# Dividing P by the row sum in the softmax's rescale, and folding the value sum straight into the projection's input, in a two-layer decode attention kernel

One core of a Trainium2 chip. The metric is the device time of one launch in microseconds (us), as the median of several runs.

## The reference, cut to what matters

Two identical layers of attention over a K/V cache and a small gated FFN, for 4 batch entries with one token each. The second layer reads the same caches and weights again.

```
B, Sq, D = 4, 1, 512;  Hq, Hkv, Sk, Dh = 32, 8, 8192, 128
def A(x, k_cache, v_cache, wq, wo):
    q = (x @ wq) as [B, Hq, 1, Dh]; k, v repeated from 8 to 32 heads
    p = softmax(q k^T * Dh**-0.5);  return (p v) as [B, 1, Hq*Dh] @ wo
x = x + A(layernorm(x), ...);  x = x + ffn(layernorm(x), ...)      # twice
```

K and V are 67 MB each. The kernel's slots (below) hold 11 to 15 MB of them, so nearly all of K and V is streamed twice.

## The kernel before

K and V come in units of 1 MB into 11 slots (later 15, when the slots of wq come free). The SP queue issues the loads in a fixed list, `ORDER`: `K` is the next K unit, `a330` the V unit of layer 0, batch 3, group 3, half 0, `b...` the same for layer 1, `c...` a V unit that both layers use. A load whose slot isn't free blocks all loads behind it. A built-in plan (`Plan.run`) takes the length of every step from a number in the source, decides in which order each engine gets its instructions and which slot a load takes, and the kernel is then emitted in that order. `PL.add(engine, us, function, dependencies, priority)` adds a step.

A K unit is transposed on VectorE (DVE, 2.31 us) and multiplied on TensorE (PE, 32 small matmuls and as many weight loads, 1.1 to 1.9 us in the traces). When all K units of one layer and batch are done, the softmax runs, and only then the V units of this layer and batch can be used and their slots be given back. "(0, 3)" stands for the pass of layer 0, batch 3 from here on.

The softmax, cut (the four blocks of scores each have their own maximum; `alpha` corrects for the common one):

```
al = PL.add("act", 0.3, g6, [s] + ex, CHAIN)             # alpha = exp(...)
def g7():                                                # rescale P, 4 DVE instructions
    for a in range(4):
        seg = pblk(q)[:, :, a, :]
        op("dve", lambda e: e.tensor_scalar(seg, seg, alpha[:, q, a:a + 1], None, op0=ALU.mult), ...)
s = PL.add("dve", 1.14, g7, [al], CHAIN)
for f in range(2):                                       # transpose P on PE, copy back
    t_ = PL.add("pe", 1.02, tr, [s, t_], CHAIN, take=f"{n}t{f}", n=16)
    evs.append(PL.add("dve" if f else "act", 0.68 if f else 1.03, ev, [t_], CHAIN, free=f"{n}t{f}"))
p_ready[(l, b)] = PL.add("act", 0.01, lambda: None, evs, CHAIN)
# beside this path: w1 (row sums, spread to 32 columns), w2 (PE matmul with ones), w3 (reciprocal -> invL)
inv_ready[(l, b)] = PL.add("dve", 0.35, w3, [s], CHAIN, free=n + "l")
```

The fold of a V group, cut:

```
op("dve", lambda e: e.transpose(blk, blk), ...)
op("dve", lambda e: e.tensor_reduce(osum[:], diag, AX.X, ALU.add), ...)
op("dve", lambda e: e.tensor_tensor(oT[:, l, heads, b], osum[:], invL[:, q, heads], ALU.mult), ...)
n = PL.add("dve", 0.17 if direct else 0.88, nm, [prev, inv_ready[(l, b)]], CHAIN, free=tag)
```

Of the kernel before, what the change touches and what calls it, by code (L numbers as in the profile page):

```python
# [5 lines left out]
ALU = mybir.AluOpType  # L6
AX = mybir.AxisListType
BF16 = mybir.dt.bfloat16
FP32 = mybir.dt.float32
# [10 lines left out]
class _Sync:  # L20
# [57 lines left out]
    def op(self, engname, fn, reads=(), writes=(), sig=True):  # L78
        self._wait(engname, self._need(reads, writes))
        ins = fn(self.eng[engname])  # L80
        if sig:
            self.count[engname] += 1
            ins.then_inc(self.prog[engname], 1)
            val = self.count[engname]
        else:
            val = self.count[engname] + 1
        self._record(engname, (self.prog[engname], val), reads, writes)
        return ins
# [184 lines left out]
NP = 2  # L273
# [7 lines left out]
def bass_interleave_layers__gqa_block_cached__swiglu_ffn__decode_kernel(  # L281
# [17 lines left out]
    REP = Hq // G  # L299
# [15 lines left out]
    with ExitStack() as es:  # L315
# [9 lines left out]
        qT1 = sb("qT1", [P, Hq * B], BF16)  # L325
        qT2 = sb("qT2", [P, Hq], BF16)
        ident = sb("ident", [P, P], BF16)
        selL = sb("selL", [P, 32], FP32)
        selw = sb("selw", [P, 32], FP32)
        invL = sb("invL", [P, NP, 32], FP32)  # L330
        xrow = pp[0:B, 0, 0:D]
        xlast = pp[0:B * NQ, 0, 0:P]
        onesm = sb("onesm", [P, P], FP32)
# [13 lines left out]
        lsum = sb("lsum", [P, NP, 4], FP32)  # L347
        gm = sb("gm", [P, 1], FP32)
        gl = sb("gl", [P, 1], FP32)
        osum = sb("osum", [P, REP], FP32)  # L350
        alpha = sb("alpha", [P, NP, 4], FP32)
        wl = sb("wl", [P, 4], FP32)
        m4 = sb("m4", [32, 4], FP32)
# [40 lines left out]

        def setup_late():
            for j in range(4):
                op("dve", lambda e: e.tensor_scalar(selL[32 * j:32 * (j + 1), :],
                                                    ident[32 * j:32 * (j + 1), 32 * j:32 * (j + 1)],
                                                    float(D), None, op0=ALU.mult),
                   reads=["ident"], writes=["selL"])  # L400

        def pk(q):
            return [f"pp{q}_{a}" for a in range(4)]
# [19 lines left out]
        def pbk(key):  # L423
            return PL.bank[key]
# [149 lines left out]
        scores_free = [None]  # L574
        p_free = {k: None for k in range(NP)}
        p_ready = {}
        inv_ready = {}

        def k_pair(u, ld, prio, prev):
            _, l, b, g, cp = u  # L580
# [37 lines left out]
        def softmax(l, b, lastq, prio):  # L618
            q = pb_of[(l, b)]
            n = f"s{l}{b}"  # L620
            ex, mx = [], None
            for a in range(4):
                def m(a=a):
                    op("dve", lambda e: e.tensor_reduce(negm[:, q, a:a + 1], bank(a), AX.X, ALU.max, negate=True),  # L624
                       reads=[f"pb{a}"], writes=[f"negm{q}_{a}"])

                def x(a=a):
                    op("act", lambda e: e.activation(pblk(q)[:, :, a, :], bank(a).rearrange("p (t j) -> p t j", j=32),  # L628
                                                     ACTF.Exp, bias=negm[:, q, a:a + 1], scale=1.0,
                                                     accum_out=lsum[:, q, a:a + 1]),  # L630
                       reads=[f"pb{a}", f"negm{q}_{a}"], writes=[f"pp{q}_{a}", f"lsum{q}_{a}"] + (pt(q) if a == 0 else []))
                mx = PL.add("dve", 0.7, m, [lastq], CHAIN)
                ex.append(PL.add("act", 0.8, x, [mx] + (p_free[q] or []), CHAIN))
            scores_free[0] = ex

            def g1():
                for c in range(4):
                    op("dve", lambda e: e.tensor_reduce(m4[:, c:c + 1], negm[32 * c:32 * (c + 1), q, :], AX.X, ALU.min),
                       reads=[f"negm{q}_{a}" for a in range(4)], writes=["m4"])
                for c in range(4):  # L640
                    op("dve", lambda e: e.tensor_reduce(gm[32 * c:32 * (c + 1), :], m4[:], AX.X, ALU.min),
                       reads=["m4"], writes=["gm"])
            s = PL.add("dve", 1.41, g1, [mx], CHAIN)

            def g6():
                op("act", lambda e: e.activation(alpha[:, q, :], negm[:, q, :], ACTF.Exp, bias=gm[:], scale=-1.0),  # L646
                   reads=[f"negm{q}_{a}" for a in range(4)] + ["gm"], writes=[f"alpha{q}"])
            al = PL.add("act", 0.3, g6, [s] + ex, CHAIN)

            def g7():  # L650
                for a in range(4):
                    seg = pblk(q)[:, :, a, :]
                    op("dve", lambda e: e.tensor_scalar(seg, seg, alpha[:, q, a:a + 1], None, op0=ALU.mult),  # L653
                       reads=[f"pp{q}_{a}", f"alpha{q}"], writes=[f"pp{q}_{a}"])
            s = PL.add("dve", 1.14, g7, [al], CHAIN)
            evs = []
            t_ = None
            for f in range(2):
                def tr(f=f):
                    bk = pbk(f"{n}t{f}")  # L660
                    stg = bank_bf(bk)
                    for t in range(8):
                        blk = f * 8 + t
                        op("pe", lambda e: e.matmul(stg[:, t * P:(t + 1) * P], lhsT=pp[:, q, blk * P:(blk + 1) * P],  # L664
                                                    rhs=ident[:], is_transpose=True, start=True, stop=True),
                           reads=pk(q) + ["ident"], writes=[f"pb{bk}"], sig=(t == 7))

                def ev(f=f):
                    bk = pbk(f"{n}t{f}")
                    src = bank_bf(bk).rearrange("p (t k r) -> p k t r", t=8, r=REP)  # L670
                    dst = pp[:, q, f * 1024:(f + 1) * 1024].rearrange("p (k t r) -> p k t r", t=8, r=REP)
                    if f == 0:
                        op("act", lambda e: e.activation(dst, src, ACTF.Copy), reads=[f"pb{bk}"], writes=[f"pt{q}_{f}"])  # L673
                    else:
                        op("dve", lambda e: e.tensor_copy(dst, src), reads=[f"pb{bk}"], writes=[f"pt{q}_{f}"])
                t_ = PL.add("pe", 1.02, tr, [s, t_], CHAIN, take=f"{n}t{f}", n=16)
                evs.append(PL.add("dve" if f else "act", 0.68 if f else 1.03, ev, [t_], CHAIN, free=f"{n}t{f}"))
            p_ready[(l, b)] = PL.add("act", 0.01, lambda: None, evs, CHAIN)

            def w1():  # L680
                op("dve", lambda e: e.tensor_tensor(wl[:], lsum[:, q, :], alpha[:, q, :], ALU.mult),
                   reads=[f"lsum{q}_{a}" for a in range(4)] + [f"alpha{q}"], writes=["wl"])
                op("dve", lambda e: e.tensor_reduce(gl[:], wl[:], AX.X, ALU.add), reads=["wl"], writes=["gl"])
                op("dve", lambda e: e.tensor_scalar(selw[:], selL[:], gl[:], None, op0=ALU.mult),  # L684
                   reads=["selL", "gl"], writes=["selw"])
            s = PL.add("dve", 0.6, w1, [al, s], CHAIN)

            def w2():
                bk = pbk(n + "l")
                op("pe", lambda e: e.matmul(ps[:, bk * BW:bk * BW + 32], lhsT=onesm[:], rhs=selw[:], start=True, stop=True),  # L690
                   reads=["onesm", "selw"], writes=[f"pb{bk}"])
            s = PL.add("pe", 0.58, w2, [s], CHAIN, take=n + "l", n=8)

            def w3():
                bk = pbk(n + "l")
                op("dve", lambda e: e.reciprocal(invL[:, q, :], ps[:, bk * BW:bk * BW + 32]),
                   reads=[f"pb{bk}"], writes=[f"invL{q}"])
            inv_ready[(l, b)] = PL.add("dve", 0.35, w3, [s], CHAIN, free=n + "l")

        opj_n = [0]  # L700
        opj_free = [None]
# [15 lines left out]
        def v_group(l, b, g, lds, prios):  # L717
# [49 lines left out]

            def nm():
                bk = pbk(tag)
                got = ps[:, bk * BW:bk * BW + REP]  # L770
                if not direct:
                    blk = ps[:, bk * BW:bk * BW + 256]
                    op("dve", lambda e: e.transpose(blk, blk), reads=[f"pb{bk}"], writes=[f"pb{bk}"])  # L773
                    diag = bass.AP(tensor=blk.tensor, offset=blk.offset, ap=[[blk.ap[0][0], P], [1, REP], [32 + REP, 8]])
                    op("dve", lambda e: e.tensor_reduce(osum[:], diag, AX.X, ALU.add), reads=[f"pb{bk}"], writes=["osum"])  # L775
                    got = osum[:]
                op("dve", lambda e: e.tensor_tensor(oT[:, l, g * REP:(g + 1) * REP, b], got,  # L777
                                                    invL[:, q, g * REP:(g + 1) * REP], ALU.mult),
                   reads=[f"pb{bk}", f"invL{q}", "osum"], writes=[f"oT{l}_{g}"])
            n = PL.add("dve", 0.17 if direct else 0.88, nm, [prev, inv_ready[(l, b)]], CHAIN, free=tag)  # L780
            if l == 0 or b == B - 1:
                wdep = [w_load[f"wo{g * REP // (Hq // 4)}"]] if l == 0 else []
                return prev, oproj(l, g, [n, opj_free[0]] + wdep + normed.get((l, g), []), prios[1])
# [281 lines left out]
```

## Time and profile before

| | before |
|---|---|
| time, median of 3 runs | 640.53 us (639.56 to 641.21) |
| span of the profiled run | 637.9 us |
| DMA, mean over the span | 257.31 MB, 403 GB/s |
| busy: PE, DVE, ACT | 63%, 64%, 6% |

How to read it: the DMA engines are busy nearly all the time and no compute engine is. So time is lost only where the stream of loads stops or slows, and before its start and after its end. The prediction shows the lines for this. What it doesn't show is the softmax that will matter. Here it is from the timeline of the kernel before (start, length, engine, line, operation, output and inputs, in brackets the idle time before and what ended it):

```profile
460.08 0.30 ACT L646 ACTIVATE alpha<-negm,gm 128x4 f32<-128x4 f32 x1
461.00 1.10 DVE L653 TENSOR_SCALAR pp<-pp,alpha 128x512 bf16<-128x512 bf16 x4
463.16 0.33 SPq L92 DMA_DIRECT2D pool<-in_A_v_cache_dram  x1
464.69 0.69 DVE L675 COPY pp<-ps 128x1024 bf16<-128x1024 bf16 x1
465.49 1.06 PE L746 MATMUL ps<-pool,pp 128*32 128x256 bf16 x32 [0.83 <-ACT pp L673]
466.20 11.36 SPq L92 DMA_DIRECT2D pool<-in_A_k_cache_dram  x6
```

From the end of alpha (460.38) to the first V matmul (465.49) it takes 5.1 us. The load queue SP stands still from 463.49 to 466.20, because its next slot holds a V unit that is waiting for this P. As soon as that V unit is used, SP goes on.

### The profile page before, as it was taken

What the parts mean: (1) busy time and instruction counts of PE and PEld (TensorE: products, weight loads), DVE (VectorE), ACT (ScalarE), POOL (GpSimd) and SP (SyncE); (2) the same over time, 40 slices, a digit from 0 to 9 for tenths busy, and PEclk for the clock granted to TensorE, in tenths of its full rate; (3) what the DMA queues carried; (4) which work ended last, traced back from release to release, by engine and by line L of the source; (5) the groups of instructions that cost most, each with busy time, mean ns of one, the idle gap of its engine ahead of it and who ended that gap; (6) DMA issues with size and microseconds to landing.
All of it is one profiled execution on the core that took longest, in us unless ns stands there. A gap on an engine that the chain in (4) does not pass through costs nothing.

```text
span 637.9 us, 18599 instructions
## 1 busy us (share of the span) xinstructions
PE 401.5 (63%) x8657; PEld 202.0 (32%) x8657; DVE 405.2 (64%) x612; ACT 40.2 (6%) x106; POOL 1.8 (0%) x8
## 2 busy tenths in 40 slices
PE   0376454375686655678565575677656776866676
PEld 0231221123542131145331241343421244721355
DVE  6386853464236958776579765466667864499732
ACT  1000200002000020000100100000100020000200
POOL 1000000000000000000000000000000000000000
PEclk9985585565556686665677677567585578577685
DMA  8999999999989999999999999999999999999991
GB/s 362 420 418 407 407 418 420 418 421 400 388 354 422 420 418 420 421 418 404 417 414 418 420 419 421 419 409 411 417 420 420 403 420 420 420 416 420 421 415 42
DMA packets 41124, 257.31 MB, mean 403 GB/s; under 512 B 3924, under 2 KB 9816, under 8 KB 11096
## 3 DMA queue, kind: packets, MB, share of 16 engines
q1 hardware_dynamic: 41048, 256.14, 97.8%
q8 instruction: 67, 1.10, 0.7%
q14 instruction: 9, 0.07, 0.0%
HBM read 256.12 MB, written 0.00 MB: 402 GB/s over the span
## 4 chain that ended last, share of the span: by engine, by line
DMA 64%; PE 16%; DVE 13%; SPq 3%; issue 2%; ACT 0%
DMA pool<-in_A_k_cache_dram 45%; DMA pool<-in_A_v_cache_dram 12%; DVE pool L589 9%; PE ps L605 8%; DMA wq_sb<-in_A_k_cache_dram 5%; PE ps L746 4%; SPq L92 3%; DMA wq_sb<-in_A_v_cache_dram 3%; PE ps L467 1%; DVE negm L624 1%; DVE wq_sb L589 1%; PE ps L792 1%; PE ps L664 1%; PE ps L845 1%; DVE ps L773 1%
## 5 line engine op out<-in xcount | busy, mean ns | idle before, releaser
L589 DVE STREAM_TRANSPOSE pool<-pool 128x2048 uint32<-128x2048 uint32 x116 | 267.1, 2308 | 88.4 <-DMA pool<-in_A_k_cache_dram 87.9
L605 PE MATMUL ps<-pool,qpad 32*32 32x512 bf16 x3840 | 197.4, 548 | 130.8 <-DVE pool L589 125.6
L605 PEld LDWEIGHTS ps<-pool,qpad 32*32 32x32 bf16 x3840 | 55.5, 110 | 248.4 <-DVE pool L589 185.8
L746 PE MATMUL ps<-pool,pp 128*32 128x256 bf16 x1952 | 100.5, 362 | 37.6 <-DMA pool<-in_A_v_cache_dram 28.9
L746 PEld LDWEIGHTS ps<-pool,pp 128*32 128x32 bf16 x1952 | 56.2, 120 | 76.3 <-DMA pool<-in_A_v_cache_dram 34.9
L773 DVE STREAM_TRANSPOSE ps<-ps 128x256 f32<-128x256 f32 x63 | 28.8, 457 | 67.4 <-PE ps L746 67.1
L628 ACT ACTIVATE pp<-ps,negm 128x512 bf16<-128x512 f32 x32 | 21.6, 686 | 322.8 <-DVE negm L624 300.5
L709 PE MATMUL ps<-oT,wo_sb 128*128 128x4 bf16 x640 | 22.4, 166 | 11.3 <-DVE oT L777 8.4
L709 PEld LDWEIGHTS ps<-oT,wo_sb 128*128 128x128 bf16 x640 | 20.0, 102 | 24.8 <-DVE oT L777 15.8
L624 DVE TENSOR_REDUCE negm<-ps 128x1 f32<-128x512 f32 x32 | 19.9, 683 | 12.4 <-PE ps L605 12.4
L467 PE MATMUL ps<-xnT,wq_sb 128*128 128x4 bf16 x640 | 18.3, 166 | 12.8 <-DMA wq_sb<-in_A_wq_dram 11.5
L467 PEld LDWEIGHTS ps<-xnT,wq_sb 128*128 128x128 bf16 x640 | 17.7, 104 | 15.3 <-DMA wq_sb<-in_A_wq_dram 11.6
L589 DVE STREAM_TRANSPOSE wq_sb<-wq_sb 128x2048 uint32<-128x2048 uint32 x8 | 18.5, 2312 | 1.8 <-DMA wq_sb<-in_A_k_cache_dram 1.8
L605 PE MATMUL ps<-wq_sb,qpad 32*32 32x512 bf16 x256 | 11.8, 492 | 9.1 <-DVE wq_sb L589 9.1
L664 PE MATMUL ps<-ident,pp 128*128 128x128 bf16 x128 | 15.4, 300 | 2.5 <-DVE oT L777 1.1
L453 ACT ACTIVATE lnv<-var,eps_sb 128x4 f32<-128x4 f32 x10 | 3.0, 297 | 221.5 <-DVE var L448 221.5
L664 PEld LDWEIGHTS ps<-ident,pp 128*128 128x128 bf16 x128 | 11.9, 137 | 9.6 <-DVE selw L684 2.9
L775 DVE TENSOR_REDUCE osum<-ps 128x4 f32<-128x32 f32 x63 | 12.1, 192 | 2.2
L777 DVE TENSOR_TENSOR oT<-osum,invL 128x4 bf16<-128x4 f32 x63 | 10.6, 169 | 2.1
L673 ACT ACTIVATE pp<-ps 128x1024 bf16<-128x1024 bf16 x8 | 8.2, 1024 | 30.1 <-PE ps L664 30.1
L845 PE MATMUL ps<-hT,wd_sb 128*128 128x4 bf16 x280 | 8.6, 166 | 1.8 <-issue 1.1
L653 DVE TENSOR_SCALAR pp<-pp,alpha 128x512 bf16<-128x512 bf16 x32 | 9.0, 344 | 1.1 <-ACT alpha L646 1.1
(68 smaller groups left out, 143.4 us busy)
## 6 DMA issues: line engine op xcount, KB each, us to landing
pool<-in_A_k_cache_dram SPq DMA_DIRECT2D x116, 1024.0 KB, 10.2
pool<-in_A_v_cache_dram SPq DMA_DIRECT2D x101, 1024.0 KB, 10.8
wq_sb<-in_A_k_cache_dram SPq DMA_DIRECT2D x8, 1024.0 KB, 14.8
wq_sb<-in_A_v_cache_dram SPq DMA_DIRECT2D x5, 1024.0 KB, 16.2
wq_sb<-in_A_wq_dram SPq DMA_DIRECT2D x1, 4096.0 KB, 20.0
wo_sb<-in_A_wo_dram SPq DMA_DIRECT2D x4, 1024.0 KB, 15.5
wg_sb<-in_B_w_gate_dram SPq DMA_DIRECT2D x2, 896.0 KB, 19.2
wu_sb<-in_B_w_up_dram SPq DMA_DIRECT2D x2, 896.0 KB, 16.9
```

What stands on the lines that cost most here:

```text
L92: ins = self.eng[engname].dma_start(out_ap, in_ap)
L467: op("pe", lambda e: e.matmul(ps[:, bk * BW + h * B:bk * BW + (h + 1) * B], lhsT=wq_sb[:, kt, h * Dh:(h + 1) * Dh], rhs=xnT[:, kt * B:(kt ...
L589: op("dve", lambda e: e.transpose(v, v), reads=keys, writes=keys)
L605: op("pe", lambda e: e.matmul(ps[32 * c:32 * (c + 1), a * BW:(a + 1) * BW], lhsT=qpad[rows, qbuf, es_, g, :], rhs=ap[h][rows, :, es_ // 2, ...
L624: op("dve", lambda e: e.tensor_reduce(negm[:, q, a:a + 1], bank(a), AX.X, ALU.max, negate=True), reads=[f"pb{a}"], writes=[f"negm{q}_{a}"])
L628: op("act", lambda e: e.activation(pblk(q)[:, :, a, :], bank(a).rearrange("p (t j) -> p t j", j=32), ACTF.Exp, bias=negm[:, q, a:a + 1], s ...
L664: op("pe", lambda e: e.matmul(stg[:, t * P:(t + 1) * P], lhsT=pp[:, q, blk * P:(blk + 1) * P], rhs=ident[:], is_transpose=True, start=True ...
L709: op("pe", lambda e: e.matmul(ps[:, OPJ * BW + nq * B:OPJ * BW + (nq + 1) * B], lhsT=wo_sb[:, h, nq * P:(nq + 1) * P], rhs=oT[:, l, h, :], ...
L746: op("pe", lambda e: e.matmul(ps[32 * n:32 * (n + 1), bk * BW:bk * BW + 256], lhsT=pp[:, q, col:col + 32], rhs=v[:, 8 * f:8 * (f + 1), 32 ...
L773: op("dve", lambda e: e.transpose(blk, blk), reads=[f"pb{bk}"], writes=[f"pb{bk}"])
L775: op("dve", lambda e: e.tensor_reduce(osum[:], diag, AX.X, ALU.add), reads=[f"pb{bk}"], writes=["osum"])
L845: op("pe", lambda e: e.matmul(ps[:, bk * BW + nq * B:bk * BW + (nq + 1) * B], lhsT=wd_sb[:, fo, nq * P:(nq + 1) * P], rhs=hT[:, fo * B:(fo ...
```

## The change

The intent: 63 folds lose their multiply by the reciprocal row sum, since P itself is divided by it. For this the row sum must be known before P is rescaled: what stood beside the path now stands on it.

```
-            def g7():
+            def w1():                        # wl = lsum * alpha; gl = sum of wl
+            s = PL.add("dve", 0.38, w1, [al], CHAIN)
+            def w2():                        # matmul(lhsT=sel, rhs=gl): the row's sum on all 4 quadrants
+            s = PL.add("pe", 0.58, w2, [s], CHAIN, take=n + "l", n=8)
+            def w3():                        # il = 1 / sum; alpha = alpha * il; then the rescale as before
...
-            s = PL.add("dve", 1.14, g7, [al], CHAIN)
+            s = PL.add("dve", 1.5, w3, [s], CHAIN, free=n + "l")
... (the old w1, w2, w3 after the transposes are gone, and selL, selw, invL with them)
-                    op("dve", lambda e: e.tensor_reduce(osum[:], diag, AX.X, ALU.add), ...)
-                op("dve", lambda e: e.tensor_tensor(oT[...], got, invL[...], ALU.mult), ...)
-            n = PL.add("dve", 0.17 if direct else 0.88, nm, [prev, inv_ready[(l, b)]], CHAIN, free=tag)
+                    op("dve", lambda e: e.tensor_reduce(dst, diag, AX.X, ALU.add), ...)      # dst is in oT, bf16
+            n = PL.add("dve", 0.17 if direct else 0.68, nm, [prev], CHAIN, free=tag)
```

`ORDER`, the list of loads, stays as it is.

More of the change, by code (lines that the diff above doesn't have):

```diff
@@ L327, in bass_interleave_layers__gqa_block_cached__swiglu_ffn__decode_kernel @@
         ident = sb("ident", [P, P], BF16)
-        selL = sb("selL", [P, 32], FP32)
-        selw = sb("selw", [P, 32], FP32)
-        invL = sb("invL", [P, NP, 32], FP32)
+        sel = sb("sel", [P, P], FP32)
         xrow = pp[0:B, 0, 0:D]
@@ L349, in bass_interleave_layers__gqa_block_cached__swiglu_ffn__decode_kernel @@
         gl = sb("gl", [P, 1], FP32)
-        osum = sb("osum", [P, REP], FP32)
+        il = sb("il", [P, 1], FP32)
         alpha = sb("alpha", [P, NP, 4], FP32)
@@ L396, in setup_late @@
             for j in range(4):
-                op("dve", lambda e: e.tensor_scalar(selL[32 * j:32 * (j + 1), :],
-                                                    ident[32 * j:32 * (j + 1), 32 * j:32 * (j + 1)],
-                                                    float(D), None, op0=ALU.mult),
-                   reads=["ident"], writes=["selL"])
+                rows = slice(32 * j, 32 * (j + 1))
+                d = ident[rows, rows]
+                rep = bass.AP(tensor=d.tensor, offset=d.offset, ap=[[d.ap[0][0], 32], [0, 4], [1, 32]])
+                op("dve", lambda e: e.tensor_copy(sel[rows, :].rearrange("p (k j) -> p k j", j=32), rep),
+                   reads=["ident"], writes=["sel"])
         def pk(q):
@@ L576, in bass_interleave_layers__gqa_block_cached__swiglu_ffn__decode_kernel @@
         p_ready = {}
-        inv_ready = {}
         def k_pair(u, ld, prio, prev):
@@ L648, in softmax @@
             al = PL.add("act", 0.3, g6, [s] + ex, CHAIN)
-            def g7():
+            def w1():
+                op("dve", lambda e: e.tensor_tensor(wl[:], lsum[:, q, :], alpha[:, q, :], ALU.mult),
+                   reads=[f"lsum{q}_{a}" for a in range(4)] + [f"alpha{q}"], writes=["wl"])
+                op("dve", lambda e: e.tensor_reduce(gl[:], wl[:], AX.X, ALU.add), reads=["wl"], writes=["gl"])
+            s = PL.add("dve", 0.38, w1, [al], CHAIN)
+            def w2():
+                bk = pbk(n + "l")
+                op("pe", lambda e: e.matmul(ps[:, bk * BW:bk * BW + 1], lhsT=sel[:], rhs=gl[:], start=True, stop=True),
+                   reads=["sel", "gl"], writes=[f"pb{bk}"])
+            s = PL.add("pe", 0.58, w2, [s], CHAIN, take=n + "l", n=8)
+            def w3():
+                bk = pbk(n + "l")
+                op("dve", lambda e: e.reciprocal(il[:], ps[:, bk * BW:bk * BW + 1]), reads=[f"pb{bk}"], writes=["il"])
+                op("dve", lambda e: e.tensor_scalar(alpha[:, q, :], alpha[:, q, :], il[:], None, op0=ALU.mult),
+                   reads=[f"alpha{q}", "il"], writes=[f"alpha{q}"])
                 for a in range(4):
@@ L678, in softmax @@
             p_ready[(l, b)] = PL.add("act", 0.01, lambda: None, evs, CHAIN)
-            def w1():
-                op("dve", lambda e: e.tensor_tensor(wl[:], lsum[:, q, :], alpha[:, q, :], ALU.mult),
-                   reads=[f"lsum{q}_{a}" for a in range(4)] + [f"alpha{q}"], writes=["wl"])
-                op("dve", lambda e: e.tensor_reduce(gl[:], wl[:], AX.X, ALU.add), reads=["wl"], writes=["gl"])
-                op("dve", lambda e: e.tensor_scalar(selw[:], selL[:], gl[:], None, op0=ALU.mult),
-                   reads=["selL", "gl"], writes=["selw"])
-            s = PL.add("dve", 0.6, w1, [al, s], CHAIN)
-            def w2():
-                bk = pbk(n + "l")
-                op("pe", lambda e: e.matmul(ps[:, bk * BW:bk * BW + 32], lhsT=onesm[:], rhs=selw[:], start=True, stop=True),
-                   reads=["onesm", "selw"], writes=[f"pb{bk}"])
-            s = PL.add("pe", 0.58, w2, [s], CHAIN, take=n + "l", n=8)
-            def w3():
-                bk = pbk(n + "l")
-                op("dve", lambda e: e.reciprocal(invL[:, q, :], ps[:, bk * BW:bk * BW + 32]),
-                   reads=[f"pb{bk}"], writes=[f"invL{q}"])
-            inv_ready[(l, b)] = PL.add("dve", 0.35, w3, [s], CHAIN, free=n + "l")
         opj_n = [0]
@@ L769, in nm @@
                 bk = pbk(tag)
-                got = ps[:, bk * BW:bk * BW + REP]
-                if not direct:
-                    blk = ps[:, bk * BW:bk * BW + 256]
-                    op("dve", lambda e: e.transpose(blk, blk), reads=[f"pb{bk}"], writes=[f"pb{bk}"])
-                    diag = bass.AP(tensor=blk.tensor, offset=blk.offset, ap=[[blk.ap[0][0], P], [1, REP], [32 + REP, 8]])
-                    op("dve", lambda e: e.tensor_reduce(osum[:], diag, AX.X, ALU.add), reads=[f"pb{bk}"], writes=["osum"])
-                    got = osum[:]
-                op("dve", lambda e: e.tensor_tensor(oT[:, l, g * REP:(g + 1) * REP, b], got,
-                                                    invL[:, q, g * REP:(g + 1) * REP], ALU.mult),
-                   reads=[f"pb{bk}", f"invL{q}", "osum"], writes=[f"oT{l}_{g}"])
-            n = PL.add("dve", 0.17 if direct else 0.88, nm, [prev, inv_ready[(l, b)]], CHAIN, free=tag)
+                dst = oT[:, l, g * REP:(g + 1) * REP, b]
+                if direct:
+                    op("dve", lambda e: e.tensor_copy(dst, ps[:, bk * BW:bk * BW + REP]),
+                       reads=[f"pb{bk}"], writes=[f"oT{l}_{g}"])
+                    return
+                blk = ps[:, bk * BW:bk * BW + 256]
+                op("dve", lambda e: e.transpose(blk, blk), reads=[f"pb{bk}"], writes=[f"pb{bk}"])
+                diag = bass.AP(tensor=blk.tensor, offset=blk.offset, ap=[[blk.ap[0][0], P], [1, REP], [32 + REP, 8]])
+                with nc.allow_low_precision(reason="the sum runs in fp32 and is rounded once"):
+                    op("dve", lambda e: e.tensor_reduce(dst, diag, AX.X, ALU.add), reads=[f"pb{bk}"],
+                       writes=[f"oT{l}_{g}"])
+            n = PL.add("dve", 0.17 if direct else 0.68, nm, [prev], CHAIN, free=tag)
             if l == 0 or b == B - 1:
```

## The prediction

> **What bounds the kernel now.** I read the page first, then eight-microsecond and one-microsecond windows, then the timeline around the one place where DMA falls off and at the end, then the timelines of the eight softmaxes. From the page: engine shares, the DMA row of the 40 slices, and the groups of instructions that the change touches.
>
> ```profile
> PE 401.5 (63%) x8657; PEld 202.0 (32%) x8657; DVE 405.2 (64%) x612; ACT 40.2 (6%) x106; POOL 1.8 (0%) x8
> DMA  8999999999989999999999999999999999999991
> DMA 64%; PE 16%; DVE 13%; SPq 3%; issue 2%; ACT 0%
> L773 DVE STREAM_TRANSPOSE ps<-ps 128x256 f32<-128x256 f32 x63 | 28.8, 457 | 67.4 <-PE ps L746 67.1
> L775 DVE TENSOR_REDUCE osum<-ps 128x4 f32<-128x32 f32 x63 | 12.1, 192 | 2.2
> L777 DVE TENSOR_TENSOR oT<-osum,invL 128x4 bf16<-128x4 f32 x63 | 10.6, 169 | 2.1
> L653 DVE TENSOR_SCALAR pp<-pp,alpha 128x512 bf16<-128x512 bf16 x32 | 9.0, 344 | 1.1 <-ACT alpha L646 1.1
> ```
>
> The reader is to see that no compute engine is full over the span, while the DMA engines are at 90% or more in all slices but the first, the twelfth and the last; 64% of the chain is DMA. The kernel streams 257.31 MB. In plain windows the rate is 420 GB/s, so the bytes alone take 612.6 us. The rest of the 637.9 us span is about 1 us before the first byte, 12 us of compute after the last, and some 12 us in which DMA runs below 420. The eight-microsecond windows show where the largest dip is, and the end:
>
> ```profile
> 176.00:184.00 8.00, 5.83 (x162) 4.98 (x162) 2.06 (x10) 0.50 (x2) 0.00 (x0) 0.50 1.02 419
> 184.00:192.00 8.00, 7.20 (x168) 3.23 (x176) 3.59 (x7) 0.00 (x0) 0.00 (x0) 0.57 0.75 284
> 192.00:200.00 8.00, 4.77 (x152) 2.23 (x130) 3.81 (x2) 0.00 (x0) 0.00 (x0) 0.85 1.01 423
> 616.00:624.00 8.00, 3.40 (x106) 2.78 (x106) 2.38 (x9) 0.00 (x0) 0.00 (x0) 0.81 0.87 358
> ```
>
> Columns after the length: busy PE, weight load, DVE, ACT, POOL, then clock, DMA share, GB/s. Between 185 and 190 us the one-microsecond windows give 229, 205, 229, 98 and 303 GB/s: 5 - 1064/420 = 2.5 us of DMA lost. It is the only hole where the queue ran dry in the middle (the other dips, at 357 to 397 GB/s, have a DMA share near 1 and lie beside the weight loads with their shorter rows). 621 to 626 loses another 2.6 us while the last transfers drain. The hole comes from the first chain: attention, FFN and query of batch 0 must finish before the K units of its second layer can be used; until then the slots are full and no load can be issued. Its timeline:
>
> ```profile
> 177.58 0.47 DVE L773 STREAM_TRANSPOSE ps<-ps 128x256 f32<-128x256 f32 x1 [2.52 <-PE ps L746]
> 178.08 0.19 DVE L775 TENSOR_REDUCE osum<-ps 128x4 f32<-128x32 f32 x1
> 178.31 0.17 DVE L777 TENSOR_TENSOR oT<-osum,invL 128x4 bf16<-128x4 f32 x1
> 178.53 0.64 PE L433 MATMUL ps<-xx,onesm 128*128 128x32 f32 x2 [1.00 <-DVE oT L777]
> ```
>
> The second layer norm (L433) takes the PSUM bank that this fold gives back, so the fold is on the path here. The tail looks as follows.
>
> ```profile
> 620.34 0.17 DVE L777 TENSOR_TENSOR oT<-osum,invL 128x4 bf16<-128x4 f32 x1
> 624.11 1.05 PE L746 MATMUL ps<-wq_sb,pp 128*32 128x256 bf16 x16 [4.07 <-DMA wq_sb<-in_A_v_cache_dram]
> 626.70 0.47 DVE L773 STREAM_TRANSPOSE ps<-ps 128x256 f32<-128x256 f32 x1 [6.20 <-PE ps L746]
> 627.63 0.17 DVE L777 TENSOR_TENSOR oT<-ps,invL 128x4 bf16<-128x4 f32 x1
> ```
>
> PE stood idle 4.07 us for the last V loads: the end is set by the stream, not by the softmax before it (597.7 to 605.8 us).
>
> **What the Trainium skill says.** "Perfetto Trace Analysis", Identifying Performance Opportunities: time is won on the most-contended engine. Here that is DMA, and the change touches no byte of it. "DMA: Bandwidth & Descriptors", Bandwidth, gives 425 GB/s for a 16 MB load; this trace has 420 to 424 in full windows, so there is no reserve. "VectorE: DVE Perf Modes", The TRN2 errata, says that an instruction has a fixed cost that small operands don't amortize; the trace agrees, since the 128x4 multiply takes 169 ns and a 128x128 cast only 273. So removing an instruction is worth its fixed cost, and an added 128x1 one costs about as much.
>
> **The change, part by part.**
> 1. Fold. 63 multiplies by the reciprocal sum go (L777). Starts are 0.23 us apart after the reduce, so a fold shrinks from 0.90 us (start of L773 to end of L777) to 0.69: 0.21 x 63 = 13 us of DVE time, 3% of its busy 405. I take the reduce into bf16 to cost the same 192 ns. The one direct group swaps a 167 ns multiply for a copy that I estimate at 135 (the 128x16 cast from PSUM, L959): 0.03 us on the tail. The multiply at 627.43 was not what the last projection waited for (the direct one at 627.63 was), so the tail gains no more.
> 2. Sum and reciprocal. Per softmax, selw (242 ns) goes and the reciprocal shrinks from 128x32 to 128x1. From 343 ns for 32 elements and 503 for 56, 6.7 ns an element, one element makes about 135 ns. A 128x4 multiply of alpha is added, 156 ns like the other 128x4 operations. Net over 8 softmaxes: -(242 + 208 - 156) x 8 = -2.4 us of DVE. The setup copies replace four 170 ns operations at about 12 us, while wq is still landing: free.
> 3. Chain. The sum now stands before the rescale of P. Added between alpha and the first rescale, without contention: two DVE operations 0.35 us (603.87 to 604.22 in the last softmax), a hop 0.05, the fp32 matmul with its return 0.68 (as L433 to L440 in the tail), reciprocal with spacing 0.17, alpha multiply 0.20: **1.45 us** later P, eight times. Contended it is more: DVE has a gap of 0.7 us between the two halves, where a K transpose of 2.31 us can slip in, and the matmul can stand behind a K unit of up to 1.95 us. I expect 1.5 to 3.5 us.
> 4. Given back. From the end of alpha to the last copy of transposed P the eight softmaxes take 13.1, 8.8, 3.5, 10.6, 6.5, 5.0, 7.0 and 3.9 us now. In at least three (the first, second and fourth) the second transposed half comes only after the reciprocal, whose bank it reuses or behind which it stands (155.40 reciprocal, 155.82 second half). With the sum first, its bank is free before the halves need theirs, so there P should be no later and may be earlier.
> 5. Order. Instructions are issued in the order of a built-in plan, which is computed anew from the changed step times, with the load order kept. Which V unit stands before which chain step, and which slot a load takes, can change by a unit (1 to 2.5 us) at any place.
>
> On the path: the hole should close by the 0.2 us of its fold; tail -0.03; every other saving of part 1 lies beside the stream. The longer softmaxes free V slots later by 1.5 to 3.5 us, but a load lands 10 to 11 us after issue (page, part 6), thus about four 2.5 us units are queued when SP has to wait, and the last softmax has 17 us of queue and 4 us of idle PE behind it. Sum of what I can place: -0.2 us. I add +0.6 for the reordering, because the load order was evidently tuned for the old step times and an arbitrary shift is likelier to open a hole than close one: 640.5 - 0.2 + 0.6, rounded to **640.9 us**.
>
> **Rivals.**
> (a) The stream hides everything: 640 to 641. For it: DMA share, 4 us of PE idle at the end, only one hole.
> (b) Later P opens holes. Each microsecond by which P comes later than the queue lasts is lost. For it: SP did run dry once, and DVE is above 90% busy in the K stretches (7.5 of 8 us), which stretches a chain with more DVE visits. Against it: none of the eight softmaxes is followed by a hole now; the dip at 185 hangs on the q chain. One or two new holes of 2 us: 643 to 646.
> (c) The lighter DVE and earlier banks bring the q chain forward and close the hole: at most 2.5 us, with smaller dips (433, 508 us) another 1: 637. Against it: the chain starts at 165.0, after the projection that waited for a weight load, and passes through V matmuls that wait for DMA.
> (d) DVE is the real bound, and its 15 us count in full: 625. Against it: DVE waits for K loads 87.9 us in total; I give this almost nothing.
>
> **Range and chances.** (a) has most of the weight, (b) about a quarter, (c) a fifth. Low end 637.5 (hole closed), high end 645 (two holes). A change of over 2% is 12.8 us: for a gain DVE would have to be the bound, or for a loss five or more holes. Faster 0.01, same 0.96, slower 0.03.
>
> **What would show it.** Folds without the multiply, 0.69 us long, and DVE busy near 390 us: part 1 and 2. From alpha to the first rescale 1.5 to 3.5 us more: part 3. Second halves of P close behind the first, so that the three long softmaxes aren't longer: part 4. DMA still at about 403 GB/s over the span, one hole near 185 of about 2.3 us, 12 us of tail: the sum. I am wrong if a hole of several microseconds follows a softmax, if the hole at 185 goes or doubles, or if the tail is no longer reached with PE waiting for DMA.

## The result, and the profile after

The changed kernel takes 643.28 us (642.06 to 643.48, 4 runs), the kernel before in the same comparison 640.87 (4 runs). The ratio is 1.0036 with a 95% interval of 1.0015 to 1.0057: slower, by less than half a per cent. Ratios are the mean time of one kernel's runs over that of the other's of the same rounds, so not quite the ratio of the medians quoted.

Three lines of the page after, the ones for busy time, the DMA row of the 40 slices, and the fold's reduce:

```profile
PE 397.5 (62%) x8657; PEld 203.6 (32%) x8657; DVE 394.3 (61%) x549; ACT 40.2 (6%) x106; POOL 1.8 (0%) x8
DMA  8999999999989999999999999999989999999991
L773 DVE TENSOR_REDUCE oT<-ps 128x4 bf16<-128x32 f32 x63 | 12.2, 194 | 2.1
```

DVE is busy 10.9 us less, nearly all of it the multiply that went (10.6), and the reduce costs the same with a bf16 output. But the DMA row has a second 8 in the middle, in the 30th slice. The eight-microsecond windows there (last three columns: granted clock, DMA share, GB/s), first before, then after:

```profile
464.00:472.00 8.00, 3.69 (x99) 2.06 (x105) 5.67 (x4) 1.02 (x1) 0.00 (x0) 0.92 1.01 420
472.00:480.00 8.00, 4.53 (x104) 1.38 (x88) 5.99 (x3) 0.00 (x0) 0.00 (x0) 0.71 1.01 419
```

```profile
464.00:472.00 8.00, 4.86 (x66) 2.60 (x50) 5.74 (x9) 1.02 (x1) 0.00 (x0) 0.50 0.81 336
472.00:480.00 8.00, 3.88 (x116) 2.10 (x112) 3.30 (x3) 0.00 (x0) 0.00 (x0) 0.92 0.82 325
```

I summed the DMA packets of both traces in one-microsecond bins and counted what is missing to 420 GB/s. The hole at 185 to 190 us is there in both, 2.47 us before and 2.44 after. A new one lies at 469 to 475, with 3.4 us lost. As all loads come in the same order, one can also ask when the same number of megabytes had arrived, counted from the start of each span (packets of the load queue):

```
MB arrived            8     96    120    168    192    200    248    256
after minus before  +0.13  +0.06  +0.76  +0.74  +1.11  +4.31  +3.60  +3.65 us
```

Of the 3.7 us between the two spans, 3.2 come in one step between 192 and 200 MB, which is the new hole. The two are level up to 96 MB; 0.7 us comes between 96 and 120 MB and 0.7 goes again between 200 and 248, in small dips.

What happened in the hole, from the timeline of the kernel after:

```profile
461.66 0.30 ACT L644 ACTIVATE alpha<-negm,gm 128x4 f32<-128x4 f32 x1
462.71 1.90 PE L603 MATMUL ps<-pool,qpad 32*32 32x512 bf16 x32 [3.77 <-DVE wl L649]
464.55 0.58 PE L656 MATMUL ps<-gl,sel 128*128 128x1 f32 x2
464.74 0.33 SPq L92 DMA_DIRECT2D pool<-in_A_v_cache_dram  x1
465.64 1.14 DVE L667 TENSOR_SCALAR pp<-pp,alpha 128x512 bf16<-128x512 bf16 x4
467.80 2.31 DVE L587 STREAM_TRANSPOSE pool<-pool 128x2048 uint32<-128x2048 uint32 x1 [1.02 <-DMA pool<-in_A_k_cache_dram]
470.04 0.65 DVE L689 COPY pp<-ps 128x1024 bf16<-128x1024 bf16 x1
470.17 1.91 PE L603 MATMUL ps<-pool,qpad 32*32 32x512 bf16 x32 [1.44 <-DVE pool L587]
472.00 1.65 PE L740 MATMUL ps<-pool,pp 128*32 128x256 bf16 x32
472.19 8.79 SPq L92 DMA_DIRECT2D pool<-in_A_k_cache_dram  x6
```

From the end of alpha (461.96) to the first V matmul it is now 10.0 us in place of 5.1. The sum's matmul (L656) stands behind a K unit on PE. After the rescale, the copy of the second half of P (L689) stands behind a K transpose on DVE, and that transpose lets a K unit onto PE ahead of the V matmul. The additional 4.9 us are 3.1 up to the rescale, 0.7 from there to the last copy, and 1.2 to the V matmul (each rounded). SP waits from 465.07 to 472.19, 7.1 us in place of 2.7, and the queued loads run out. What ended this wait shows in the list of SP's waits from 440 to 482 us (us in total, times, longest):

```profile
SPq L62 <- PE ps L603: 22.3, 6, 7.1
SPq L62 <- PE ps L740: 12.4, 9, 2.5
```

The wait of 7.1 us ended with a K unit (L603, done at 472.08) and not with a V unit. While P is not there, the V units keep their slots, and the first slot to come free is that of a K unit which landed behind them: it was transposed at 467.80 and multiplied at 470.17, ahead of the V units on PE. In the kernel before, a V unit came first, and its slot ended the wait.

### The profile page after: what moved, and what is told of

Its sections match the earlier page's. It is cut to its first block, busy times and chain, and to the rows that moved or that the text cites. A ratio compares the mean times of both kernels' runs of the same rounds, so it can differ in the third digit from the quotient of the medians. Undisturbed runs are those within 1.5% of the kernel's fastest.

```text
span 641.6 us, 18536 instructions
## 1 busy us (share of the span) xinstructions
PE 397.5 (62%) x8657; PEld 203.6 (32%) x8657; DVE 394.3 (61%) x549; ACT 40.2 (6%) x106; POOL 1.8 (0%) x8
## 4 chain that ended last, share of the span: by engine, by line
DMA 64%; PE 17%; DVE 13%; SPq 3%; issue 2%; ACT 0%
DMA pool<-in_A_k_cache_dram 45%; DMA pool<-in_A_v_cache_dram 12%; DVE pool L587 10%; PE ps L603 9%; DMA wq_sb<-in_A_k_cache_dram 5%; PE ps L740 4%; SPq L92 3%; DMA wq_sb<-in_A_v_cache_dram 3%; DVE negm L622 1%; PE ps L466 1%; DVE wq_sb L587 1%; PE ps L787 1%; PE ps L678 1%; PE ps L840 1%; PE ps L703 0%
## 5 line engine op out<-in xcount | busy, mean ns | idle before, releaser
L603 PE MATMUL ps<-pool,qpad 32*32 32x512 bf16 x3840 | 193.0, 537 | 135.0 <-DVE pool L587 116.8
L603 PEld LDWEIGHTS ps<-pool,qpad 32*32 32x32 bf16 x3840 | 56.3, 109 | 247.9 <-DVE pool L587 171.2
L740 PE MATMUL ps<-pool,pp 128*32 128x256 bf16 x1952 | 101.7, 365 | 40.2 <-DMA pool<-in_A_v_cache_dram 31.6
L740 PEld LDWEIGHTS ps<-pool,pp 128*32 128x32 bf16 x1952 | 56.9, 121 | 77.6 <-DMA pool<-in_A_v_cache_dram 37.1
L603 PE MATMUL ps<-wq_sb,qpad 32*32 32x512 bf16 x256 | 11.8, 496 | 8.8 <-DVE wq_sb L587 8.8
L773 DVE TENSOR_REDUCE oT<-ps 128x4 bf16<-128x32 f32 x63 | 12.2, 194 | 2.1
L689 DVE COPY pp<-ps 128x1024 bf16<-128x1024 bf16 x8 | 5.4, 676 | 11.8 <-PE ps L678 11.8
L787 PEld LDWEIGHTS ps<-xnT,wu_sb 128*128 128x128 bf16 x280 | 8.2, 104 | 4.4 <-issue 1.7
## 6 DMA issues: line engine op xcount, KB each, us to landing
pool<-in_A_k_cache_dram SPq DMA_DIRECT2D x116, 1024.0 KB, 10.6
pool<-in_A_v_cache_dram SPq DMA_DIRECT2D x101, 1024.0 KB, 10.9
```

The source lines that it names most:

```text
L603: op("pe", lambda e: e.matmul(ps[32 * c:32 * (c + 1), a * BW:(a + 1) * BW], lhsT=qpad[rows, qbuf, es_, g, :], rhs=ap[h][rows, :, es_ // 2, ...
L740: op("pe", lambda e: e.matmul(ps[32 * n:32 * (n + 1), bk * BW:bk * BW + 256], lhsT=pp[:, q, col:col + 32], rhs=v[:, 8 * f:8 * (f + 1), 32 ...
L787: op("pe", lambda e: e.matmul(ps[:, bk * BW + (fo - f0) * B:bk * BW + (fo - f0 + 1) * B], lhsT=w_sb[:, kt, fo * P:(fo + 1) * P], rhs=xnT[: ...
```

## The experiments

The theory to be tested (A): a later P of (0, 3) alone costs the time, by holding V slots while the load queue drains. Rival B: the shorter fold shifted the planned order, and that made the hole. Rival C: the load list is tuned to the old step times, so any changed step opens holes somewhere. The built-in plan's own clock turned out to show the new hole too. (`Plan.run`, run from the sources without a chip, gives 630.0 us for the kernel before and 633.8 for the changed one; but it also gives 634.0 for fold_only below, which on the chip took 1.4 us more than the kernel before.) What counts below is the chip. The first four kernels ran together on one chip, the last four on another, each set beside 11 runs of the kernel before (median 640.21 us in both).

### The softmax part alone

```
-                    op(..., e.tensor_reduce(dst, diag, AX.X, ALU.add), ...)
+                    op(..., e.tensor_reduce(osum[:], diag, AX.X, ALU.add), ...)
+                op("dve", lambda e: e.tensor_tensor(oT[...], got, one[:], ALU.mult), ...)   # one: all 1.0
-  0.17 if direct else 0.68
+  0.17 if direct else 0.88
```

> The softmax part of the change alone: the sum stands before the rescale, but every fold keeps its multiply (by ones), at its old length, also in the built-in plan. Result stays correct. Theory A (P of the softmax of layer 0, batch 3 comes later, its V slots come free later, the load queue runs dry once): 643 to 645 us, and the dry spell near 470 us stays, about 3 us. Theory B (the shorter fold shifted the order of the instructions and that opened the dry spell): 640 to 641.5, no dry spell near 470.

642.46 us (641.91 to 644.17), ratio 1.0030 (1.0014 to 1.0047). One window of its trace:

```profile
464.00:472.00 8.00, 4.85 (x72) 2.95 (x76) 6.62 (x9) 1.02 (x1) 0.00 (x0) 0.50 0.75 311
```

The hole is there (2.66 us). DVE is busy 404.4 us, about as much as before (405.2): putting the whole saving back did not make it slower than the changed kernel. The time lies a little under the range that A expected. B is out as the cause of this hole.

### The fold part alone, in a newly planned and in the old order

```
 before, the fold:  oT <- reduce, no multiply; P is not divided (wrong result on purpose)
 fold_only:         0.68 for the fold in the plan, dependency on the reciprocal dropped
 fold_same_order:   the same instructions, but the plan keeps 0.88 and the dependency
```

> The fold part alone: folds write their sum straight to the projection's input, the softmax is as before (wrong result on purpose: nobody divides by the row sum). Theory A: no dry spell near 470, 640 to 641. Theory B: the dry spell near 470 is there, 643 to 645. Theory C (the load order is tuned to the old step times, and any changed step time reorders units and opens dry spells somewhere): 643 to 645 with dry spells elsewhere; the plan's own clock has three of together 3.6 us in the stretch that it calls 543 to 555, some 10 us later in the trace.

> The same folds without the multiply, but the plan is told the old step time and the old dependencies, so that every instruction stands where it stood before (wrong result on purpose). All theories agree that the faster fold alone, in the old order, costs nothing: 640 to 641, at best 0.2 to 0.5 below the kernel before. If it is slower by more than 1 us, the faster fold itself does harm. If fold_only is slower than this, the order and not the work does it (theory C).

Both results are wrong. fold_only took 641.62 us (640.38 to 643.20), ratio 1.0009 (0.9992 to 1.0026). The time lies between what A (640 to 641) and C (643 to 645) expected. There is no hole near 470, but its profiled run (643.2 us, its slowest) has four dips between 548 and 563 us, 3.2 us lost in all, and another 1.3 us lost at 322 to 329. One window:

```profile
552.00:560.00 8.00, 6.99 (x210) 5.56 (x210) 4.23 (x12) 0.50 (x2) 0.00 (x0) 0.50 0.95 314
```

fold_same_order took 639.96 us (638.79 to 640.54), ratio 0.9986 (0.9970 to 1.0002), without new holes. So the faster fold is harmless, and what it may give is at most a quarter of a per cent and not clear of noise. For rival C: the same work in a newly planned order shows other dips in the trace and is 1.7 us slower by the medians. Against the kernel before neither is clear of noise, but against each other they are: five of the six runs of fold_only lie above all six of fold_same_order, and the means are 1.8 us apart, 3.7 standard errors. So a new order alone can cost time. It did not make the hole near 470.

### All of the change but one softmax

The change in seven softmaxes and their folds; (0, 3) keeps the old form with the multiply in its folds:

```
+NEW = [(l, b) for l in range(2) for b in range(4) if (l, b) != (0, 3)]
+            if (l, b) in NEW: (the new w1, w2, w3)   else: (g7, and the old w1, w2, w3)
```

> The change in seven of the eight softmaxes and their folds; the softmax of layer 0, batch 3 in the form of before, its folds with the multiply. Theory A: no dry spell near 470, 640 to 642 us. If the later P costs a little in every softmax instead: 643, with the dry spell or with small losses spread out.

639.93 us (639.42 to 641.93), ratio 0.9994 (0.9976 to 1.0012).

```profile
464.00:472.00 8.00, 5.08 (x98) 2.60 (x105) 5.67 (x4) 0.94 (x1) 0.00 (x0) 0.71 1.02 421
```

No hole. Seven changed softmaxes cost nothing that can be seen; the eighth makes the loss. This order is newly planned too, so "any changed step opens holes", C in its strong form, doesn't hold. But not all of the seven hold their V units back: from alpha to the first V matmul only two of them, the third and the last, take over 0.5 us more than before (2.8 and 2.0 us), and three take 0.9 to 2.1 us less. The run shows that delays of 2 to 3 us at these two places are covered, not at all seven. DVE is busy 396.0 us here, 9 us less than before, and the time is still that of before.

### Nothing but a detour in this one softmax

The kernel before, with w1, w2 and w3 inserted ahead of the rescale of (0, 3), their result unused:

```
+            if (l, b) in [(0, 3)]:
+                s = PL.add("dve", 0.38, n1, [al], CHAIN)
+                s = PL.add("pe", 0.58, n2, [s], CHAIN, take=n + "d", n=8)
+                s = PL.add("dve", 1.5, n3, [s], CHAIN, free=n + "d")      # reciprocal, a multiply into scratch, then g7
-            s = PL.add("dve", 1.14, g7, [al], CHAIN)
```

> The kernel before, its folds as they were, with nothing but a detour on the path of one softmax (layer 0, batch 3): the same two DVE steps, matmul and reciprocal ahead of the rescale, their result unused, so it is correct. Theory A: this delay alone makes a dry spell of about 3 us near 470, and 642.5 to 644 us. If it takes the rest of the change (shorter folds, the sum in the other seven), it stays at 640 to 641.

643.42 us (641.69 to 645.33), ratio 1.0044 (1.0024 to 1.0064).

```profile
464.00:472.00 8.00, 5.25 (x68) 2.96 (x52) 5.97 (x13) 1.02 (x1) 0.00 (x0) 0.50 0.88 367
472.00:480.00 8.00, 3.66 (x104) 1.99 (x104) 3.57 (x2) 0.00 (x0) 0.00 (x0) 0.90 0.80 302
```

The hole is there (2.88 us; the profiled run is the slowest of its six, 645.33 us), with none of the rest of the change but other small buffers and setup copies. The detour in one softmax of eight is enough for the whole loss.

### The delay in doses

Two kernels take part of the delay away, in (0, 3) alone, from the changed kernel:

```
 act03, act_sa03:  second half of P copied by ACT in place of DVE (no wait behind a K transpose)
 act_sa03 only:    +  scores_free[0] = ex + [s]     # the next pass's first K unit waits for the sum's matmul
```

> The changed kernel, and in the softmax of layer 0, batch 3 alone the second transposed half of P is copied by ACT instead of DVE, so that it no longer waits behind a K transpose. Theory A in doses: P comes earlier by part of the delay, the dry spell near 470 shrinks from 3.4 us (2.66 in chain_only) to about 2.3, time 642 to 642.5. If the DVE queue is the whole cause, the dry spell goes.

> As act03, and the first K unit of the next pass has to wait for the sum's matmul, so that this doesn't stand behind it on TensorE. What is left of the delay is the detour's own length of about 1.45 us. Theory A: the dry spell near 470 shrinks to 1.0 to 1.6 us, time 640.8 to 641.8; the slip-ins of a K unit and a K transpose are then worth about 2 of the 3.4 us.

act03: 641.48 us (640.84 to 642.37), ratio 1.0013 (0.9995 to 1.0030). act_sa03: 640.79 us (639.34 to 642.61), ratio 1.0006 (0.9986 to 1.0026). One window of each, act03 first:

```profile
464.00:472.00 8.00, 5.39 (x91) 3.42 (x99) 5.97 (x7) 1.94 (x2) 0.00 (x0) 0.53 0.88 345
```

```profile
464.00:472.00 8.00, 5.40 (x110) 2.84 (x107) 4.62 (x2) 1.94 (x2) 0.00 (x0) 0.71 1.01 413
```

| kernel | end of alpha to first V matmul of (0, 3), us | SP stood still, us | lost near 470, us | time, us |
|---|---|---|---|---|
| before | 5.1 | 2.7 | 0 | 640.21 |
| old03 | 5.6 | 3.2 | none found | 639.93 |
| act_sa03 | 6.6 | 3.3 | none found | 640.79 |
| act03 | 8.0 | 6.0 | 2.4 | 641.48 |
| changed kernel | 10.0 | 7.1 | 3.4 | 643.28 (beside 640.87) |
| detour03 | 10.0 | 7.1 | 2.9 | 643.42 |
| chain_only | 10.6 | 7.2 | 2.7 | 642.46 |

Up to 10 us the loss goes with the delay; the last three have nearly the same standstill and lose 2.7 to 3.4 us in one profiled run each, so a difference of 0.7 us is not explained. For act_sa03 I had expected 1.0 to 1.6 us of hole to be left; there was none. For act03 the hole was as expected and the time 0.5 us under its range (642 to 642.5). So the detour's own length (the first 1.5 us of delay) is covered by the queue, and the loss comes from the K unit and the K transpose that get in between. The times of act03 and act_sa03 are not clear of the kernel before; the holes in the traces carry this step.

### Two loads moved

The changed kernel, with the V loads of (0, 3) that would sit and wait asked for two K loads later:

```
-         "b131 b111 K a330 a310 K K a360 K K K K K K a361 ...
+         "b131 b111 K K K a330 a310 a360 K K K K K K a361 ...
```

> The changed kernel with two tokens of its load order moved: the two V loads of layer 0, batch 3 that are in the slots when its softmax runs (a330 and a310) are asked for after two more K loads. Nothing else is changed. If the dry spell near 470 comes from V units that sit in slots until the later P is ready, two K units that can be used and given back at once stand there instead, the dry spell goes, and the time falls by about 3 us to 639.5 to 641. If the time was lost in the longer softmax itself or spread out, it stays at 643.

639.91 us (639.42 to 640.89), ratio 0.9992 (0.9976 to 1.0008).

```profile
464.00:472.00 8.00, 5.29 (x130) 2.93 (x114) 4.06 (x8) 1.02 (x1) 0.00 (x0) 0.95 1.02 422
```

```profile
459.95 0.30 ACT L644 ACTIVATE alpha<-negm,gm 128x4 f32<-128x4 f32 x1
465.29 6.87 SPq L92 DMA_DIRECT2D pool<-in_A_k_cache_dram  x5
469.39 1.06 PE L740 MATMUL ps<-pool,pp 128*32 128x256 bf16 x32 [0.83 <-ACT pp L687]
```

P is still late here: 9.1 us from the end of alpha (460.25) to the V matmul. But SP goes on at 465.29, four microseconds before that matmul, since the slot it needs is now given back by a K unit that was loaded earlier and doesn't wait for P. SP stood still only 1.9 us. The hole is gone, with nothing changed in the softmax. That rules out a loss in the longer softmax itself. It is also the best form of the change that I found: correct, and level with the kernel before, not faster than it.

One thing stays open. All variants but fold_same_order are newly planned, so the later P and the plan's answer to it (a K unit ahead of the V unit on PE) were not taken apart. In the changed kernel P was ready at 470.69. Had the first V unit gone then, it would by my estimate (half of the 1.65 us of L740) have been done at about 471.5 in place of the K unit's 472.08, so that order is worth about 0.6 of the 3.4 us.

## Why the prediction was right, and where it was not

The range and the class held: 643.28 us lies in 637.5 to 645, and the difference is within 2%. The central figure of 640.9 was 2.4 us low. The account behind it, rival (a), did not hold: one of the signs that I had named for being wrong, "a hole of several microseconds follows a softmax", is what happened. That the time still lies in the range is due to the range's width, which took in rival (b). By its own steps:

- **What bounds the kernel.** Right. 10.9 us of DVE work went and the time did not fall; chain_only has the work back and is not slower than the changed kernel. The page "Perfetto Trace Analysis" of the Trainium skill, Optimization Strategy, says to find the gaps on the most-contended engine and what blocks it there; here the new loss was such a gap, the 3.4 us of DMA at 469. Some details were misread: the first load's bytes come at 1.8 us, not 1, and not all small dips lie beside weight loads (504 to 512 us, 397 GB/s, does not).
- **Part 1, the fold.** Nearly right: the reduce costs 194 ns, and at the hole near 185 the layer norm's matmul starts 0.75 us after the fold's start in place of 0.95. The 0.2 us that this should take from the hole can't be seen (2.47 to 2.44). The copy of the direct group takes 168 ns (135 estimated), no less than the multiply it replaced (167). "DVE busy near 390" was off (394.3), since I had subtracted start-to-start times, and the gaps between instructions were never counted as busy.
- **Part 2.** Nearly: the reciprocal of 128x1 takes 162 ns (135 estimated), the multiply of alpha 229 (156 estimated). By the groups of DVE instructions the net over eight softmaxes is -1.5 us (-2.4 estimated).
- **Part 3, the chain.** Mostly right. From the end of alpha to the first rescale the eight softmaxes take 3.4, 2.8, 1.8, 0.6, 2.4, 3.1, 2.3 and 1.4 us more, 2.2 in the mean; 1.5 to 3.5 was expected, and two lie below. In the undisturbed last one it is 1.4 (1.45 estimated). But "later P, eight times" did not come: up to the first V matmul the eight take 0.3, 0.1, 2.0, -2.5, -0.3, 4.9, 0.2 and 1.4 us more, so only three are much later.
- **Part 4, what is given back.** Right: the three long softmaxes take 13.3, 8.9 and 7.6 us from alpha to the last copy (13.1, 8.8 and 10.6 before). The second half doesn't follow closely in all of them: in the first softmax its copy still ends 4.5 us after that of the first half.
- **The step that failed** is the sum: "about four 2.5 us units are queued when SP has to wait", so that 1.5 to 3.5 us would be absorbed everywhere. First, the delay was counted only up to the rescale. In (0, 3) it grows to 4.9 us until a V unit is used, as a K transpose and a K unit slip in behind it. Second, the queue's reserve was taken from the median time from issue to landing. At this softmax SP had last issued at 464.74 and the stream fell off at 469.5, so the queue lasted under 5 us, about two units and not four, of which the kernel before already used 2.7. The doses bear this out: 1.5 us more delay (SP stood still 3.3 us) did no harm, 2.9 more (6.0 us) did.
- **Rivals.** What happened is rival (b), "one or two new holes of 2 us: 643 to 646", to which I gave about a quarter. It came as one hole of 3.4 us, at the softmax that I had listed with a delay of 5.0 and not singled out. Its time was right and its place was not foreseen.
- **The +0.6 for reordering.** fold_only and fold_same_order show that a newly planned order can open other dips and cost some 1.7 us. old03 and v_later, newly planned too, cost nothing. In the changed kernel the 0.6 is not what made the loss.

## What to carry to other kernels

In a kernel that is bound by its stream, ask of a change what it does to the moment at which buffers come free, at the one place where the load queue has least reserve. A median latency says nothing of that place: read when the queue's issuer stood still, for how long, and for which buffer. And if a step must become later, move the loads that wait for it before undoing the step: two moved tokens gave back all of the 3 us here. And where a program has a model of its own timing, run it on the changed source before predicting: here it showed 3.7 us where 2.4 were measured, though it also showed 4.0 for fold_only, where 1.4 were measured and not clear of noise.

## What the Trainium skill lacked or had wrong

- "Perfetto Trace Analysis", What "DMA-bound" means, lists single DMA engines, the sequencer and SBUF reads as what binds. It lacks the case: a queue that runs dry once because slots hold data that waits for a result (3.4 us lost, DMA at 336 and 325 GB/s in two windows). Its "consistent bubbles" are about gaps that repeat; this one came once.
- "VectorE: DVE Perf Modes", Scalar operands, doesn't say what a per-partition scalar costs: multiplying 128x4 by a 128x1 operand took 229 ns, by a constant 158 (qscale), the tensor-by-tensor multiply of 128x4 145.
- "DMA: Bandwidth & Descriptors", Where 436 GB/s comes from, says without a condition that for HBM to SBUF the HBM side (about 358 GB/s) binds. Here 256 MB came from HBM at 420 GB/s in undisturbed windows and 403 over the whole span, on one core alone, which fits the 425 that the same page measured. The note under that measurement has the condition that the sentence lacks: both cores of the HBM domain streaming.
